# T5 attention followed by a feed-forward layer on one core: longer rows for q and k, full-width matmuls outside the scores, a band table through DRAM, paired score units and interleaved FFN products

## The chip, the cores and the metric

The kernel runs on one core of one Trainium2 chip. The metric is the device time of one execution in microseconds (us), lower is better. "TensorE", "VectorE", "ScalarE", "GpSimd" and "SyncE" are the engines; the profile writes PE, DVE, ACT, POOL and SP for them, and PEld for TensorE's weight loads. DRAM is the memory that holds the inputs, SBUF the on-chip memory that the engines work from, and PSUM the one that TensorE writes its products to; a DMA is a transfer, here between DRAM and SBUF or within SBUF. FFN is the feed-forward layer. "Before" and "after" are the two kernels.

## The reference

```python
# q, k, v: 8 batches x 8 heads x 576 tokens x 64; bias_table: 32 buckets x 8 heads
scores = (1/sqrt(64)) * q @ k^T
n      = abs(i - j)                      # distance of the two tokens
bucket = n if n < 16 else min(31, 16 + int(log(n/16)/log(128/16) * 15))
scores = scores + bias_table[bucket]     # one value per head and distance
attn   = exp(scores - rowmax);  attn = attn / rowsum
x      = attn @ v                        # -> 4608 tokens x 512
h      = x @ w_in                        # 512 -> 2048
g      = max(0.01 * h, h)                # leaky ReLU
out    = g @ w_out                       # 2048 -> 512, float32
```

Two properties matter. The bias is constant from distance 128 on, so after dividing by the constant it is a factor in a band of 128 tokens on each side of the diagonal and 1 elsewhere. And the 576 tokens are four blocks of 128 and one tail of 64, which is where narrow matmuls come from.

## The kernel before

Work goes by head pair: 32 pairs, numbered 0 to 31 here, four per batch. A pair has six score units (four blocks of 128 keys, one for the last 64 queries, one for the last 64 keys of both heads), an exponential on ScalarE per unit, a multiplication by the band table `eb` on VectorE, and two products with V ("AV"), one per head. The FFN is cut into 288 pieces of four 512-column matmuls, which are woven between the attention's matmuls, eight per pair.

The q and k loads take one token row of one head (64 numbers) at a time:

```python
    def load(b, h0, h1, by_head):
        i = b % NBUF
        for src, dst in ((q, qn[i]), (k, kn[i])):
            ...
                for c in range(NJ):
                    nc.gpsimd.dma_start(
                        out=dst[:, c, h0 * D : h1 * D].rearrange("s (h d) -> s h d", d=D),
                        in_=src[b, h0:h1, c * P : (c + 1) * P, :].rearrange("h s d -> s h d"),
                    )
        ...                                            # tails of 64 tokens apart; v likewise
```

The band table is built in 8 partitions, one per head, and spread from there to 128 partitions, each one element further to the left. The weights come after the loads of batch 0, and batch 1 comes after the weights:

```python
    ub = per.tile([H, UW], BF16, name="ub")            # 8 partitions x 512
    nc.vector.memset(ub, 1.0)
    ...                                                # 17 copies fill the band
    for h in range(H):
        r = ub[h : h + 1, :]
        eng = nc.sync if h % 2 == 0 else nc.scalar
        eng.dma_start(
            out=eb[:, h, :],
            in_=bass.AP(tensor=r.tensor, offset=r.offset + P - 1,
                        ap=[list(r.ap[0]), [-1, P], [1, 3 * P]]),
        )
    for e in range(2):
        nc.sync.dma_start(out=eb4[e * SL : (e + 1) * SL, :, :], in_=eb[0:SL, e::2, 0 : P + SL])
```

Score units use half of TensorE's rows (a head has 64 dimensions). Transposes of q and x, and AV, have a narrow last step for the tail:

```python
        nc.tensor.transpose(ps[:, NJ * P : S], in_=qn[i][0:SL, NJ, cols], identity=ident[0:SL, 0:SL])
    ...
            for e in range(2):                         # a score unit: two half-row matmuls
                r = slice(e * D, (e + 1) * D)
                nc.tensor.matmul(ps[:, e, :], lhsT=kt[r, u * P : (u + 1) * P], rhs=qt[r, 0:512],
                                 start=True, stop=True)
            nc.scalar.activation(at[:, :, u, 0:512], ps, AF.Exp, scale=scale)
    ...
        for ic in range(NJ + 1):                       # AV
            m = P if ic < NJ else SL
            cols = slice(ic * P, ic * P + m)
            for c in range(NJ):
                nc.tensor.matmul(ps[0:m, ic, :], lhsT=at[:, e, c, cols], rhs=vn[i][:, c, 2 * p + e, :],
                                 start=(c == 0), stop=False)
            nc.tensor.matmul(ps[0:m, ic, :], lhsT=at4[:, cols], rhs=v4[i][:, p, e, :],
                             start=False, stop=True)
```

The order of a pair, with `moe(k)` taking the next k pieces of the FFN from one queue (all of a tile's first product, then all of its second):

```python
        if p == 1 and b + 1 < B:
            load(b + 1, 0, H, False)
        if n == 0:
            load_weights()
        for u in range(NJ + 2):
            if n < N:
                qk_unit(n, u)
                band(n, u)
            if u == 1 and n > 0:
                av(n - 1, 0)
                moe(1)
            elif u == 3 and n > 0:
                av(n - 1, 1)
                moe(1)
            elif u == 4:
                moe(1)
                if n + 1 < N:
                    transposes(n + 1)
            elif u == 5:
                moe(1)
                if n > 0:
                    x_transposes(n - 1)
                    finished(n - 1)
            else:
                moe(2)
    moe(10 ** 9)
```

The softmax here doesn't subtract the row's maximum and nothing guards it: scores larger than these inputs give would overflow.

## Time and profile before

| | |
|---|---|
| time, median (lowest to highest) | 483.45 us (482.1 to 485.69), 4 runs |
| span of the profiled run | 481.7 us |
| first FFN matmuls and full TensorE from | about 85 us |
| steady time per head pair | 12.14 us |

The page of the kernel before opens with busy time per engine. In its second part a digit is the busy share, in tenths, of one of 40 slices of 12 us; the third part counts DMA packets, megabytes, and the share of all 16 DMA engines' time.

```profile
span 481.7 us, 9029 instructions
PE 427.3 (89%) x3808; PEld 214.1 (44%) x3808; DVE 193.6 (40%) x577; ACT 248.3 (52%) x338; POOL 122.5 (25%) x161
...
PE   2106837999999999999999999999999999999996
...
q0 software_dynamic: 115632, 18.36, 54.9%
```

TensorE comes and goes for the first 84 us and is full from there on. Its idle time is in the start.

Two stretches of the same kernel, the start and a steady pair. The columns are the stretch, its length, busy time with the number of instructions for PE, PEld, DVE, ACT and POOL, then the granted TensorE clock, the DMA share and GB/s.

```profile
0.00:85.00 85.00, 34.56 (x372) 19.47 (x372) 27.69 (x102) 26.80 (x32) 47.96 (x69) 0.90 1.51 113
182.00:194.33 12.33, 12.33 (x120) 6.18 (x117) 5.90 (x18) 9.04 (x14) 0.32 (x1) 1.00 0.50 50
```

TensorE works 34.56 of the first 85 us, while the DMA engines are busy (the DMA share reads 1.51; it is a sum over transfers and can pass 1). In the steady state it has no idle time, while ScalarE has 9.04 and VectorE 5.90 of 12.33 us. So a change in the steady state pays only if it shortens TensorE's own time.

From the chain of waits of the kernel before, the two longest DMAs that hold the start and one that follows them (start, duration, what):

```profile
11.42 27.23 DMA qn_100<-in_q_dram
...
48.40 19.92 DMA w_out_sb<-in_moe_w_out_dram
...
71.20 4.97 DMA kn_1_105<-in_k_dram
```

The last line is the tail of batch 1's k, which is issued behind the weights. Batch 1's q is too, and TensorE waits for it (in square brackets, the idle time before the matmul and what ended it):

```profile
69.20 0.29 PE L213 MATMUL ps_tq<-ident,qn_101 128*128 128x128 bf16 x1 [5.06 <-DMA qn_101<-in_q_dram]
```

From the timeline of TensorE before, around one pair. The columns are start, modelled duration, engine, line, operation, out<-in, rows*columns of the array in use, shape of the moving operand, count. Durations overlap, so the starts are what to read.

```profile
189.69 0.19 PE L287 MATMUL ps_o<-v_1_109,at_1979 128*128 128x65 bf16 x1
189.82 0.31 PE L285 MATMUL ps_o<-vn_107,at 128*64 128x65 bf16 x4
189.96 0.20 PE L287 MATMUL ps_o<-v_1_109,at_1979 128*64 128x65 bf16 x1
190.09 0.39 PE L313 MATMUL pm_2273<-xT_92,w_in_sb 128*128 128x512 bf16 x1
...
192.16 0.39 PE L213 MATMUL ps_tq<-ident,qn_101 128*128 128x128 bf16 x4
192.48 0.20 PE L214 MATMUL ps_tq<-ident,qn_101 64*128 64x64 bf16 x1
192.61 0.40 PE L219 MATMUL ps_tk<-ident,kn_103 128*128 128x128 bf16 x4
...
194.01 0.52 PE L302 MATMUL ps_tx<-ident,opair 128*128 128x128 bf16 x5
194.34 0.41 PE L237 MATMUL ps_s<-qt,kt 64*128 64x512 bf16 x2
```

Consecutive 65-column matmuls of the same width start 0.03 us apart. From the last 128*128 one (189.69) to the first 128*64 one (189.82) it is 0.13 us, and again 0.13 us on leaving (189.96 to 190.09). So each change of the array's width costs about 0.1 us beyond the streaming. The q tail shows it twice: four transposes of 128 columns stream in about 0.22 us, yet the 64*128 one starts 0.32 us after them, and 0.13 us passes until the next full one.

Two marks give the steady time per pair. These are the starts of the same matmul (score unit 5) of pairs 8 and 31 before; (411.35 - 132.07) / 23 = 12.14 us.

```profile
132.07 0.38 PE L251 MATMUL ps_s<-qt,kt 128*128 128x512 bf16 x1
...
411.35 0.38 PE L251 MATMUL ps_s<-qt,kt 128*128 128x512 bf16 x1
```

### The profile page before, as it was taken

What the parts mean: (1) busy time and instruction counts of PE and PEld (TensorE: products, weight loads), DVE (VectorE), ACT (ScalarE), POOL (GpSimd) and SP (SyncE); (2) the same over time, 40 slices, a digit from 0 to 9 for tenths busy, and PEclk for the clock granted to TensorE, in tenths of its full rate; (3) what the DMA queues carried; (4) which work ended last, traced back from release to release, by engine and by line L of the source; (5) the groups of instructions that cost most, each with busy time, mean ns of one, the idle gap of its engine ahead of it and who ended that gap; (6) DMA issues with size and microseconds to landing.
All of it is one profiled execution on the core that took longest, in us unless ns stands there. A gap on an engine that the chain in (4) does not pass through costs nothing.

```text
span 481.7 us, 9029 instructions
## 1 busy us (share of the span) xinstructions
PE 427.3 (89%) x3808; PEld 214.1 (44%) x3808; DVE 193.6 (40%) x577; ACT 248.3 (52%) x338; POOL 122.5 (25%) x161
## 2 busy tenths in 40 slices
PE   2106837999999999999999999999999999999996
PEld 0003514455555544555454555545555555544442
DVE  3102624444544454445444544454445444401101
ACT  1303624774477447754675467546754675152340
POOL 9127349506200721072107120703000000000000
PEclk9999876999999999999999999999999999999999
DMA  6999999909360926091809170927001000101101
GB/s 35 46 61 133 198 178 138 90 1 121 59 59 1 121 55 62 1 121 48 69 1 118 51 69 1 105 64 68 1 21 41 30 2 5 63 22 42 47 17 72
DMA packets 122817, 29.37 MB, mean 61 GB/s; under 512 B 114584, under 2 KB 117656, under 8 KB 122776
## 3 DMA queue, kind: packets, MB, share of 16 engines
q0 software_dynamic: 115632, 18.36, 54.9%
q1 hardware_dynamic: 6568, 10.03, 7.4%
q10 hardware_dynamic: 576, 0.39, 1.8%
q8 instruction: 30, 0.49, 0.4%
q14 instruction: 11, 0.09, 0.1%
HBM read 36.70 MB, written 9.44 MB: 96 GB/s over the span
## 4 chain that ended last, share of the span: by engine, by line
PE 82%; DMA 11%; POOL 4%; DVE 1%; issue 1%; ACT 1%; POOLq 0%
PE ps_o L285 10%; PE ps_s L237 7%; DMA qn_100<-in_q_dram 6%; DMA w_out_sb<-in_moe_w_out_dram 4%; PE ps_tx L302 2%; PE ps_o L287 2%; PE ps_tk L219 2%; PE ps_s L251 1%; PE ps_s L244 1%; PE ps_tq L213 1%; DMA kn_1_105<-in_k_dram 1%; PE pm_5235 L320 1%; PE pm_4729 L320 1%; PE pm_4043 L320 1%; PE pm_3880 L320 1%; PE pm_3357 L320 1%
## 5 line engine op out<-in xcount | busy, mean ns | idle before, releaser
L239 ACT ACTIVATE at<-ps_s 128x1024 bf16<-128x1024 f32 x128 | 129.4, 1022 | 72.2 <-PE ps_s L237 58.5
L271 DVE TENSOR_TENSOR at<-at,eb 128x768 bf16<-128x768 bf16 (+2 forms) x128 | 65.0, 508 | 135.4 <-ACT at L239 107.4
L320 PEld LDWEIGHTS <-gt 128*128 128x128 bf16 x576 | 49.8, 98 | 58.4 <-issue 6.0
L313 PEld LDWEIGHTS <-w_in_sb 128*128 128x128 bf16 x576 | 49.5, 98 | 58.5 <-issue 7.2
L285 PEld LDWEIGHTS <-at 128*128 128x128 bf16 (+1 forms) x1280 | 55.1, 102 | 23.4 <-issue 11.0
L237 PE MATMUL ps_s<-qt,kt 64*128 64x512 bf16 x256 | 52.2, 407 | 12.2 <-ACT at L239 10.5
L292 DVE TENSOR_TENSOR opair<-ps_o,rcp 128x256 bf16<-128x256 f32 (+1 forms) x128 | 41.0, 320 | 4.4
L285 PE MATMUL ps_o<-vn_106,at 128*128 128x65 bf16 (+1 forms) x640 | 34.7, 200 | 3.2 <-DVE opair L292 3.2
L291 DVE RECIPROCAL rcp<-ps_o 128x4 f32<-128x4 f32 (+1 forms) x128 | 21.0, 164 | 37.0 <-PE ps_o L287 37.0
L237 PEld LDWEIGHTS <-kt 64*128 64x128 bf16 x256 | 12.7, 95 | 50.4 <-issue 47.6
L285 PE MATMUL ps_o<-vn_107,at 128*128 128x65 bf16 (+1 forms) x640 | 32.8, 195 | 0.0
L111 POOL DMA_DIRECT2D qn_101<-in_q_dram x16 | 14.1, 896 | 67.2 <-PE ps_tq L214 61.7
L246 ACT ACTIVATE at<-ps_s 128x512 bf16<-128x512 f32 x32 | 19.1, 596 | 18.3 <-PE ps_s L244 18.3
L213 PE MATMUL ps_tq<-ident,qn_100 128*128 128x128 bf16 x64 | 7.5, 237 | 21.5 <-DMA qn_100<-in_q_dram 21.5
L111 POOL DMA_DIRECT2D qn_100<-in_q_dram x16 | 14.1, 926 | 45.7 <-PE ps_tk L220 22.9
L216 DVE COPY qt<-ps_tq 128x576 bf16<-128x576 bf16 x32 | 14.6, 456 | 26.3 <-PE ps_tq L214 26.3
L222 DVE COPY kt<-ps_tk 128x640 bf16<-128x640 bf16 x32 | 15.7, 490 | 8.0 <-PE ps_tk L220 8.0
L302 PEld LDWEIGHTS <-opair 128*128 128x128 bf16 (+1 forms) x160 | 12.9, 99 | 10.9 <-issue 0.5
L302 PE MATMUL ps_tx<-ident,opair 128*128 128x128 bf16 (+1 forms) x160 | 17.1, 220 | 0.0
L134 POOL DMA_DIRECT2D vn_107<-in_v_dram x16 | 14.1, 894 | 12.0 <-PE ps_o L287 11.5
L213 PEld LDWEIGHTS <-qn_100 128*128 128x128 bf16 x64 | 5.1, 104 | 25.1 <-DMA qn_100<-in_q_dram 17.1
L134 POOL DMA_DIRECT2D vn_106<-in_v_dram x16 | 14.0, 897 | 7.9 <-PE ps_o L287 7.4
(978 smaller groups left out, 772.8 us busy)
## 6 DMA issues: line engine op xcount, KB each, us to landing
out_dram<-y SPq DMA_DIRECT2D x36, 256.0 KB, 2.1
w_in_sb<-in_moe_w_in_dram POOLq DMA_DIRECT2D x4, 512.0 KB, 8.9
w_out_sb<-in_moe_w_out_dram POOLq DMA_DIRECT2D x4, 512.0 KB, 17.1
qn_101<-in_q_dram POOLq DMA_DIRECT2D x16, 128.0 KB, 4.2
kn_103<-in_k_dram POOLq DMA_DIRECT2D x16, 128.0 KB, 4.0
vn_107<-in_v_dram POOLq DMA_DIRECT2D x16, 128.0 KB, 4.3
qn_100<-in_q_dram POOLq DMA_DIRECT2D x12, 128.0 KB, 4.0
kn_102<-in_k_dram POOLq DMA_DIRECT2D x12, 128.0 KB, 4.2
```

The source lines that it names most:

```text
L111: nc.gpsimd.dma_start(out=dst[:, c, h0 * D : h1 * D].rearrange("s (h d) -> s h d", d=D), in_=src[b, h0:h1, c * P : (c + 1) * P, :].rearran ...
L134: nc.gpsimd.dma_start(out=vn[i][:, c, h0:h1, 0:D], in_=v[b, h0:h1, c * P : (c + 1) * P, :].rearrange("h s d -> s h d"),)
L237: nc.tensor.matmul(ps[:, e, :], lhsT=kt[r, u * P : (u + 1) * P], rhs=qt[r, 0:512], start=True, stop=True)
L239: nc.scalar.activation(at[:, :, u, 0:512], ps, AF.Exp, scale=scale)
L246: nc.scalar.activation(at[:, :, :, 512:S], ps[:, :, 0 : NJ * SL].rearrange("p e (c i) -> p e c i", i=SL), AF.Exp, scale=scale)
L271: nc.vector.tensor_tensor(out=o, in0=o, in1=m, op=ALU.mult)
L285: nc.tensor.matmul(ps[0:m, ic, :], lhsT=at[:, e, c, cols], rhs=vn[i][:, c, 2 * p + e, :], start=(c == 0), stop=False)
L291: nc.vector.reciprocal(rcp[0:rows, cs, :], ps[0:rows, cs, D : D + 1])
L292: nc.vector.tensor_tensor(out=opair[0:rows, cs, e * D : (e + 1) * D], in0=ps[0:rows, cs, 0:D], in1=rcp[0:rows, cs, :].to_broadcast([rows, ...
L302: nc.tensor.transpose(ps[:, ic * P : ic * P + m], in_=opair[0:m, ic, :], identity=ident[0:m, 0:m])
L313: nc.tensor.matmul(pm, lhsT=w_in_sb[:, c, f * P : (f + 1) * P], rhs=xT[c][:, t0 : t0 + TT], start=(c == 0), stop=(c == n_cc - 1))
L320: nc.tensor.matmul(pm, lhsT=gt[:, f, ts * P : (ts + 1) * P], rhs=w_out_sb[:, f, :], start=(f == 0), stop=(f == n_fc - 1))
```

## The change

Six things were changed together, all meant to raise TensorE's share. q and k are loaded six tokens per row, 384 contiguous numbers, so a batch needs 1,536 packets instead of 9,216; VectorE then puts the two heads of a pair side by side and undoes the token order when it copies the transposes out of PSUM. Outside the scores no matmul uses fewer than 96 of the array's rows: AV's last step reads 128 columns and the surplus is never used. The band table is built in all 128 partitions, written to DRAM, and read back with each partition's row one element further. Score units are issued two at a time. And the FFN's first product of one tile alternates, piece by piece, with the second product of another. The sixth is small in the code: batch 1's q and k are now issued ahead of the weights.

```diff
-    def load(b, h0, h1, by_head):
+    def load_qk(b, h0, h1):
         i = b % NBUF
+        for src, dst in ((q, qn[i]), (k, kn[i])):
+            nc.gpsimd.dma_start(
+                out=dst[0:RQ, h0:h1, :, :].rearrange("r h c d -> r h (c d)"),      # RQ = 96
+                in_=src[b, h0:h1, :, :].rearrange("h (r c) d -> r h (c d)", c=NC), # NC = 6
+            )
  ... (load_v keeps the old form; kn4 and its fill are gone)

-    ub = per.tile([H, UW], BF16, name="ub")
+    ub = per.tile([P, H, UW], BF16, name="ub")
     nc.vector.memset(ub, 1.0)
  ... (the same copies, now on 128 partitions x 8 heads)
-    for h in range(H):
-        r = ub[h : h + 1, :]
-        eng = nc.sync if h % 2 == 0 else nc.scalar
-        eng.dma_start(out=eb[:, h, :], in_=bass.AP(tensor=r.tensor, offset=r.offset + P - 1,
-                        ap=[list(r.ap[0]), [-1, P], [1, 3 * P]]))
+    urows = nc.dram_tensor("u_rows", [P, H, UW], BF16, kind="Internal")
+    for h0, h1 in ((0, 2), (2, H)):
+        nc.sync.dma_start(out=urows.ap()[:, h0:h1, :], in_=ub[:, h0:h1, :])
+    for h0, h1 in ((0, 2), (2, H)):
+        nc.sync.dma_start(
+            out=eb[:, h0:h1, :],
+            in_=bass.AP(tensor=urows, offset=h0 * UW + P - 1, ap=[[H * UW - 1, P], [UW, h1 - h0], [1, 3 * P]]),
+        )
  ... (eb4 likewise from urows)

+    def pair_rows(n, which):                           # VectorE: the two heads of a pair side by side
+        t = pr_pool.tile([RQ, NC, 2 * D], BF16, name="pr")
+        nc.vector.tensor_copy(out=t.rearrange("r c (e d) -> r c e d", e=2),
+                              in_=src[b % NBUF][0:RQ, 2 * p : 2 * p + 2, :, :].rearrange("r e c d -> r c e d"))
+    def transpose_q(n):
+        for c in range(NC):
+            nc.tensor.transpose(ps[:, c * RQ : (c + 1) * RQ], in_=qs[0:RQ, c, :],
+                                identity=ident[0:RQ, 0:RQ])
+        nc.vector.tensor_copy(out=qt.rearrange("p (r c) -> p r c", c=NC),
+                              in_=ps[:, 0:S].rearrange("p (c r) -> p r c", c=NC))
  ... (transpose_k likewise)

         for ic in range(NJ + 1):                       # AV
-            m = P if ic < NJ else SL
-            cols = slice(ic * P, ic * P + m)
             for c in range(NJ):
-                nc.tensor.matmul(ps[0:m, ic, :], lhsT=at[:, e, c, cols], rhs=vn[i][:, c, 2 * p + e, :],
+                o = (e * NJ + c) * S + ic * P
+                nc.tensor.matmul(ps[:, ic, :], lhsT=at[:, o : o + P], rhs=vn[i][:, c, 2 * p + e, :],
                                  start=(c == 0), stop=False)
  ... (the step with at4 likewise; x_transposes without its narrow tail)

+            if n == 0:                                 # order of the first loads
+                load_qk(1, 0, H)
+                load_weights()
+                load_v(1, 0, H, False)
+            ps_a, ps_b = qk_mm(n, 0), qk_mm(n, 1)      # score units in pairs
+            exp_band(n, 0, ps_a)
+        moe(1)
+        if live:
+            exp_band(n, 1, ps_b)
  ... (units 2, 3 and 4, 5 likewise)

     def moe(n_pieces):
-        while queue and n_pieces: ... next(queue[0]) ...
+        for _ in range(n_pieces):
+            piece(("in", "out")[turn], False)          # skipped when that product has nothing ready
+            turn ^= 1
```

## The prediction

> **What bounds the kernel now.** Three stretches (table by stages, timeline). (1) 0 to about 85 us, start-up: TensorE waits. The chain of waits runs here through DMAs: the batch-0 q load (27 us), the w_out load (20 us), the batch-1 k tail (5 us). The first exponentials start at 18.2 us, because ScalarE was issuing band-table DMAs; TensorE is busy 0.8 of 10 us in 30-40. Batch-1 q and k land at 69 to 76 us behind the weights. (2) 85 to 412 us, steady state: TensorE is busy 12.33 of 12.33 us per head pair (182-194.33), ScalarE 9.0, VectorE 5.9, clock 1.00. (3) 412 to 482 us: FFN alone, 3.45 us per 16 matmuls, 216 ns each.
>
> **What the steady state consists of.** Eight FFN pieces of 4 x 216 ns are 6.9 us of about 12.2; attention takes 5.3. Reading starts of neighbouring matmuls: a pair of half-row score matmuls streams in 0.22 us but occupies 0.32, with about 0.1 us lost going in and again coming out. The same 0.1 us appears around the 64-column attention-times-V matmuls and the 64-row transposes. The Trainium skill ("TensorEngine Tiling (Array Packing)", Key Properties) says changing the tiling mode drains TensorE; the trace agrees, at about 0.1 us. I count about 17 such changes per head pair: 5 score groups (10), two AV tails (4), q tail (2), x tail (1).
>
> **What the change does.** Changes fall from 17 to 6 (three score groups), saving about 1.1 us per head pair. Streaming work stays: six 96-column transposes replace four 128s and a tail. Steady state: 12.2 to about 11.1 us, TensorE-bound. VectorE gains pair-row copies and strided q/k copies; I estimate 7 us of 11, off the critical path. Interleaving both FFN products evens ScalarE (4 instead of 0 or 8 leaky-ReLU passes) but removes no TensorE work; during the first tile only 4 pieces per pair run, leaving 78 instead of about 56 to 64 for the tail.
>
> Start-up: q and k go from 9,216 packets of 64 elements per batch to 1,536 of 384. The 256-byte reads ran at about 1,000 packets per us (24,269 in 70 to 94 us), so a batch takes 14 us now, about 10 to 12 then. The band table no longer comes from single SBUF partitions (16.8 us to landing) and ScalarE issues none of it; but VectorE must build it on 128 partitions (the fill alone about 4 us, estimated from 0.48 us for 512 elements), then out and back through DRAM: first bands about 18 us. Then about 6.6 us per pair; batch 1's v lands behind the weights, estimated 52 to 57 us. So the steady phase begins near 53 instead of 85 us.
>
> **Sum.** 53 + 4 pairs x 8 + 23 x 11.1 + last pair 9 + 78 x 0.865 + 3.5 = 420; plus 5 for new stalls: **425 us**, range 410 to 446. Faster by over 2%: 0.96; within 2%: 0.03; slower: 0.01.
>
> **What would show it.** Steady pair 11.1 us with TensorE full; no gap around AV; queue-0 packets near 52,000; first FFN matmul near 50 us; tail about 70 us of 216 ns matmuls.
>
> **What would make it wrong.** 96-row transposes draining too (+0.4 us a pair, +13 us); VectorE lateness (strided copies, larger ops) stalling TensorE through the three shared PSUM buffers, one now held by the interleaved second product; the DRAM round trip landing after 25 us; batch 1's v after 65 us.

## The result and the profile after

| | before | after |
|---|---|---|
| time, median (lowest to highest) | 483.45 us (482.1 to 485.69) | 439.62 us (439.09 to 439.96) |
| ratio, 95% | | 0.9088 (0.9053 to 0.9124) |

There were four runs of each. A ratio is the mean time of one kernel's runs over that of the other's of the same rounds, so it is not quite the ratio of the medians. The result is right.

The page after, same lines:

```profile
span 438.2 us, 9059 instructions
PE 392.3 (90%) x3872; PEld 202.3 (46%) x3872; DVE 229.1 (52%) x581; ACT 247.1 (56%) x338; POOL 60.8 (14%) x84
...
PE   0511888999999999999999999999999999999996
...
q0 software_dynamic: 52960, 18.36, 37.6%
```

The same 18.36 MB went through the load queue in less than half the packets (a slice is now 11 us). TensorE is at 0.8 from the fifth slice (44 us) on and full from about 77 us; before, it came and went until 84 us. The stages of the kernel after:

```profile
0.00:68.50 68.50, 29.06 (x386) 17.23 (x386) 39.04 (x115) 26.94 (x32) 28.15 (x43) 1.00 1.14 165
68.50:102.40 33.90, 31.48 (x405) 18.14 (x405) 24.45 (x63) 28.29 (x40) 6.06 (x9) 1.00 0.52 54
281.50:292.60 11.10, 11.10 (x120) 5.74 (x119) 6.75 (x17) 7.40 (x11) 0.00 (x0) 1.00 0.28 55
366.00:438.20 72.20, 68.13 (x316) 30.71 (x314) 8.30 (x12) 19.07 (x32) 0.00 (x0) 1.00 0.13 48
```

The steady pair is again 11.10 of 11.10 us TensorE, with VectorE's longer copies (6.75 us, from 5.90) still far from the limit. The last stretch is 79 pieces of the FFN (316 matmuls) and nothing else.

Where the time went, by the starts of score unit 5 of pairs 4, 8 and 31 in the two profiled runs:

| stretch | before | after | difference |
|---|---|---|---|
| start to pair 4 | 83.5 | 65.5 | -18.0 |
| pair 4 to 8 | 48.5 | 34.6 | -14.0 |
| pair 8 to 31 (23 pairs) | 279.3 | 253.8 | -25.4 |
| pair 31 to the end | 70.4 | 84.3 | +13.9 |
| span | 481.7 | 438.2 | -43.5 |

The second and fourth rows cancel. With alternating products a pair gives the FFN only four pieces while the first tile's second product is not ready, so 16 pieces of 0.865 us = 13.8 us leave pairs 5 to 8 and come back at the end. The gain is the start, 18 us, and the steady state, 25.4 us.

The marks of pairs 9 and 31 after, 243.36 us apart, 11.062 us per pair. (Before, by the same two marks, it was 12.141.)

```profile
110.56 0.39 PE L253 MATMUL ps_s<-qt,kt_109 128*128 128x512 bf16 x1
...
353.92 0.39 PE L253 MATMUL ps_s<-qt,kt_109 128*128 128x512 bf16 x1
```

The timeline of TensorE after, in a steady pair:

```profile
284.31 0.61 PE L244 MATMUL ps_s<-qt,kt_109 64*128 64x512 bf16 x4
284.85 0.39 PE L327 MATMUL pm_4181<-xT_92,w_in_sb 128*128 128x512 bf16 x1
...
286.34 0.29 PE L301 MATMUL ps_o<-vn_104,at_110 128*128 128x65 bf16 x4
286.47 0.19 PE L303 MATMUL ps_o<-v_0_106,at_0_112 128*128 128x65 bf16 x1
286.50 0.42 PE L227 MATMUL ps_tk<-ident,pr 96*128 96x96 bf16 x6
286.75 1.03 PE L338 MATMUL pm_4097<-w_out_sb,gt 128*128 128x512 bf16 x4
```

AV's last step runs on at 0.03 us per matmul. The 96-row transposes start 0.03 us after it, and the next 512-column matmul starts 0.25 us later, which is their streaming time (6 x 96 columns): no width change is visible around 96 rows. The four half-row matmuls of two units take 0.54 us with one change behind them.

From the chain of waits after, the start (start, duration, what):

```profile
4.15 3.47 DVE ub L156
...
11.56 8.22 DMA u_rows<-ub
...
21.51 20.77 DMA eb_99<-u_rows
```

And from the waits after, the two that VectorE's band multiplications spent on the table (engine, tile, line <- releaser: total us, count, mean):

```profile
DVE at_110 L288 <- DMA eb<-u_rows: 14.0, 1, 14.0
DVE at_0_112 L288 <- DMA eb_99<-u_rows: 9.9, 1, 9.9
```

The start is now held by the table's way through DRAM: filled at 7.6 us, finished at 11.2, written by 19.8 (1 MB, while q, k and v are arriving), read back by 28.9 for the first two heads and by 42.3 for the tail table `eb4` (shown as `eb_99`). What the reads met between 30 and 42 us is shown by the DMA queues of that window (packets, MB, share of 16 engines). q0 carries the weights, q1 the table.

```profile
q0 software_dynamic: 1203, 1.95, 87.4%
q1 hardware_dynamic: 1164, 0.66, 25.0%
```

Nearly equal numbers of packets went through, but one of q0's is on average three times as large. The Trainium skill ("DMA: Bandwidth & Descriptors", Queues, rings and completion order) says that each DMA engine takes turns between queue rows packet by packet. The equal counts agree with turns (in the trace a packet is about one contiguous row: 52,960 packets for 51,712 rows of q, k, v and weights; the page's holds several descriptors). So the table, with short rows, got 0.66 of the 2.61 MB beside the weights.

### The profile page after: what moved, and what is told of

It reads as the page before. It is cut to its first block, busy times and chain, and to the rows that moved or that the text cites. A ratio compares the mean times of both kernels' runs of the same rounds, so it can differ in the third digit from the quotient of the medians.

```text
span 438.2 us, 9059 instructions
## 1 busy us (share of the span) xinstructions
PE 392.3 (90%) x3872; PEld 202.3 (46%) x3872; DVE 229.1 (52%) x581; ACT 247.1 (56%) x338; POOL 60.8 (14%) x84
## 3 DMA queue, kind: packets, MB, share of 16 engines
q0 software_dynamic: 52960, 18.36, 37.6%
## 4 chain that ended last, share of the span: by engine, by line
PE 79%; DVE 7%; DMA 7%; ACT 5%; issue 2%; SPq 0%; DVEq 0%; ACTq 0%
PE ps_o L301 7%; PE ps_s L244 6%; DMA eb_99<-u_rows 5%; PE ps_s L253 2%; DMA u_rows<-ub 2%; PE ps_o L303 2%; ACT at_110 L264 2%; ACT at_111 L264 2%; PE ps_tx L315 2%; PE ps_tq L216 1%; PE ps_tk L227 1%; PE ps_s L250 1%; DVE at_110 L288 1%; DVE opair L307 1%; ACT gt L329 1%
## 5 line engine op out<-in xcount | busy, mean ns | idle before, releaser
L264 ACT ACTIVATE at_111<-ps_s 128x1024 bf16<-128x1024 f32 x64 | 64.7, 1021 | 38.4 <-PE ps_s L244 38.3
L264 ACT ACTIVATE at_110<-ps_s 128x1024 bf16<-128x1024 f32 x64 | 64.3, 1021 | 20.6 <-PE ps_s L244 20.4
L288 DVE TENSOR_TENSOR at_110<-at_110,eb 128x512 bf16<-128x512 bf16 (+1 forms) x64 | 32.3, 506 | 53.0 <-ACT at_110 L264 36.8
L288 DVE TENSOR_TENSOR at_111<-at_111,eb 128x512 bf16<-128x512 bf16 (+1 forms) x64 | 32.3, 506 | 44.1 <-ACT at_111 L264 40.0
L244 PE MATMUL ps_s<-qt,kt_109 64*128 64x512 bf16 x128 | 20.8, 396 | 13.7 <-DVE kt_109 L230 13.1
L301 PEld LDWEIGHTS <-at_110 128*128 128x128 bf16 x640 | 28.3, 100 | 10.0 <-DVE opair L307 3.0
L307 DVE TENSOR_TENSOR opair<-ps_o,rcp 128x320 bf16<-128x320 f32 x64 | 31.5, 492 | 2.2
L301 PEld LDWEIGHTS <-at_111 128*128 128x128 bf16 x640 | 27.2, 98 | 9.9 <-DVE opair L307 3.0
L216 PE MATMUL ps_tq<-ident,pr 96*128 96x96 bf16 x192 | 14.2, 212 | 11.5 <-DVE pr L208 11.5
L244 PE MATMUL ps_s<-qt,kt_108 64*128 64x512 bf16 x128 | 21.6, 403 | 2.3 <-DVE kt_108 L230 1.2
L303 PE MATMUL ps_o<-v_0_106,at_0_112 128*128 128x65 bf16 x80 | 13.7, 200 | 8.9 <-DVE at_0_112 L288 8.8
L303 PEld LDWEIGHTS <-at_0_112 128*128 128x128 bf16 x160 | 15.9, 99 | 9.2 <-DVE at_0_112 L288 9.2
L306 DVE RECIPROCAL rcp<-ps_o 128x5 f32<-128x5 f32 x64 | 12.2, 191 | 11.4 <-PE ps_o L303 11.4
L244 PEld LDWEIGHTS <-kt_109 64*128 64x128 bf16 x128 | 4.2, 94 | 28.1 <-issue 13.8
L301 PE MATMUL ps_o<-vn_104,at_110 128*128 128x65 bf16 x320 | 15.8, 200 | 0.9 <-DVE opair L307 0.8
L123 POOL DMA_DIRECT2D vn_105<-in_v_dram x16 | 14.1, 888 | 15.5 <-PE ps_o L303 7.6
L301 PE MATMUL ps_o<-vn_104,at_111 128*128 128x65 bf16 x320 | 14.5, 194 | 1.7 <-DVE opair L307 1.7
L216 PEld LDWEIGHTS <-pr 96*128 96x128 bf16 x192 | 10.0, 101 | 12.5 <-DVE pr L208 12.4
L303 PEld LDWEIGHTS <-at_1_113 128*128 128x128 bf16 x160 | 15.6, 97 | 0.2 <-DVE at_1_113 L288 0.2
```

Of the source, the lines that this page charges most:

```text
L123: nc.gpsimd.dma_start(out=vn[i][:, c, h0:h1, 0:D], in_=v[b, h0:h1, c * P : (c + 1) * P, :].rearrange("h s d -> s h d"),)
L216: nc.tensor.transpose(ps[:, c * RQ : (c + 1) * RQ], in_=qs[0:RQ, c, :], identity=ident[0:RQ, 0:RQ])
L288: nc.vector.tensor_tensor(out=o, in0=o, in1=m, op=ALU.mult)
L301: nc.tensor.matmul(ps[:, ic, :], lhsT=at[:, o : o + P], rhs=vn[i][:, c, 2 * p + e, :], start=(c == 0), stop=False)
L303: nc.tensor.matmul(ps[:, ic, :], lhsT=at4[:, ic * P : (ic + 1) * P], rhs=v4[i][:, p, e, :], start=False, stop=True)
L306: nc.vector.reciprocal(rcp, ps[:, :, D : D + 1])
```

## The experiments

Each kernel is the kernel after with the edit shown. All gave right results, and each was timed in three rounds against the kernel before on the same chip (four runs of it, seven or eight of before). "Ratio" is to before; after has 0.9088. The experiments ran in groups on two chips, so between groups the ratios are compared. Differences from after that are given in us are between medians; by the ratios they come out 0.4 to 1.2 us higher.

| kernel | median us (lowest to highest) | ratio, 95% |
|---|---|---|
| one_unit | 447.97 (447.88 to 448.17) | 0.927 (0.9248 to 0.9293) |
| tails64 | 458.2 (458.15 to 458.52) | 0.9482 (0.9463 to 0.9502) |
| old_packets | 439.27 (438.26 to 441.48) | 0.9095 (0.9064 to 0.9127) |
| old_band | 451.94 (451.63 to 452.84) | 0.9354 (0.9333 to 0.9376) |
| band_first | 426.74 (425.94 to 427.12) | 0.8834 (0.882 to 0.8848) |
| band_first_short | 439.88 (439.66 to 440.45) | 0.911 (0.9097 to 0.9124) |
| no_mix | 439.2 (439.06 to 439.77) | 0.9097 (0.9083 to 0.911) |
| band_first_v | 426.96 (426.52 to 428.48) | 0.8851 (0.8831 to 0.8872) |
| band_early | 430.44 (429.8 to 430.63) | 0.8908 (0.8887 to 0.893) |
| band_early_fill | 432.43 (430.94 to 433.31) | 0.8951 (0.8917 to 0.8985) |
| band_early_v | 420.09 (418.18 to 421.44) | 0.8694 (0.8656 to 0.8733) |
| band_early_v_fill | 418.95 (418.59 to 419.96) | 0.8675 (0.8648 to 0.8703) |

### The steady state: one_unit and tails64

The theory is that each change of the array's width costs 0.1 us of TensorE and that the whole steady gain is the number of changes taken away. The rival is that the gain comes from something else in the steady state, such as ScalarE being fed better. `one_unit` issues the score units singly again (two more groups, so four more changes per pair):

```diff
-            ps_a, ps_b = qk_mm(n, 0), qk_mm(n, 1)
-            exp_band(n, 0, ps_a)
+            exp_band(n, 0, qk_mm(n, 0))
         moe(1)
         if live:
-            exp_band(n, 1, ps_b)
+            exp_band(n, 1, qk_mm(n, 1))
  ... (units 2 and 3 likewise)
```

> The changed kernel with its score units issued one at a time again; all other parts stay. Theory (mode changes): four more changes of the tiling mode per head pair at about 0.1 us each, with TensorE still busy without a break: the steady pair goes from 11.09 to about 11.5 us, the time up by 9 to 14 us. Rival (the pairs matter because they keep ScalarE fed, not because of TensorE's modes): matmul streaming stays at 11.1 us a pair and TensorE shows idle time waiting for ScalarE, or, if that wait was hidden before, the time changes by less than 3 us.

`tails64` brings back the 64-token tails of AV and of the x transposes (six more changes per pair), and with them VectorE's normalisation in two calls:

```diff
         for ic in range(NJ + 1):
+            m = P if ic < NJ else SL
...
-                nc.tensor.matmul(ps[:, ic, :], lhsT=at[:, o : o + P], rhs=vn[i][:, c, 2 * p + e, :],
+                nc.tensor.matmul(ps[0:m, ic, :], lhsT=at[:, o : o + m], rhs=vn[i][:, c, 2 * p + e, :],
...
-            nc.tensor.transpose(ps[:, ic * P : (ic + 1) * P], in_=opair[:, ic, :], identity=ident)
+            nc.tensor.transpose(ps[:, ic * P : ic * P + m], in_=opair[0:m, ic, :], identity=ident[0:m, 0:m])
```

> The changed kernel with 64-column attention-times-V matmuls and the 64-row x transpose put back for the last 64 tokens (and VectorE's normalisation split in two calls as it was before). Theory: six more mode changes per head pair at 0.1 us: steady pair about 11.7 us, time up by 13 to 19 us. Rival (a narrower matmul does less work, and what costs is only the number of matmuls): no change or slightly faster, within 3 us, since the number of matmuls is the same.

Measured: one_unit is 8.4 us slower than after, tails64 18.6 us slower. The marks of pairs 9 and 31 in one_unit:

```profile
109.10 0.39 PE L253 MATMUL ps_s<-qt,kt 128*128 128x512 bf16 x1
...
361.81 0.39 PE L253 MATMUL ps_s<-qt,kt 128*128 128x512 bf16 x1
```

And in tails64:

```profile
113.96 0.39 PE L253 MATMUL ps_s<-qt,kt 128*128 128x512 bf16 x1
...
371.38 0.39 PE L253 MATMUL ps_s<-qt,kt 128*128 128x512 bf16 x1
```

The pair takes 252.71 / 22 = 11.487 us in one_unit, 0.425 more than after, so 0.106 per change; and 257.42 / 22 = 11.701 us in tails64, 0.639 more, so 0.1065 per change. Two edits of different kind give the same price per change. Nor does TensorE wait for ScalarE: in the steady pairs of both (240 to 270 us) its timeline shows no wait for another engine. So the theory stands. The total of one_unit is a little below what was expected because pairs 5 to 8, which TensorE does not fill, are faster with single units: 8.05 us each against 8.48 after, where the timeline shows the paired units waiting 0.26 to 0.31 us for ScalarE to free a score buffer. The steady loss of 23 x 0.425 = 9.8 us less 4 x 0.43 = 1.7 us is 8.1 us.

### The start: old_packets and old_band

Each undoes one half of what was changed in the start. `old_packets` loads q and k in rows of 64 numbers again, into the same places:

```diff
-            nc.gpsimd.dma_start(
-                out=dst[0:RQ, h0:h1, :, :].rearrange("r h c d -> r h (c d)"),
-                in_=src[b, h0:h1, :, :].rearrange("h (r c) d -> r h (c d)", c=NC),
-            )
+            for c in range(NC):
+                nc.gpsimd.dma_start(
+                    out=dst[0:RQ, h0:h1, c, :],
+                    in_=src[b, h0:h1, :, :].rearrange("h (r c) d -> r h c d", c=NC)[:, :, c, :],
+                )
```

> The changed kernel with the same row layout of q and k, but loaded in 64-element pieces again (six transfers for each one). Packets of queue 0 go from about 53,000 to about 114,000. Theory (after the change, the start is held by the band table and not by q and k): steady pair unchanged at 11.1 us, the first steady pair starts a few us later, time up by 3 to 10 us. Rival (the long rows are what shortened the start): the start goes back to about 85 us, time up by 15 us or more.

`old_band` builds and spreads the table as the kernel before does:

```diff
-    ub = per.tile([P, H, UW], BF16, name="ub")
+    ub = per.tile([H, UW], BF16, name="ub")
...
-    urows = nc.dram_tensor("u_rows", [P, H, UW], BF16, kind="Internal")
-    ... (two writes, two reads)
+    for h in range(H):
+        r = ub[h : h + 1, :]
+        eng = nc.sync if h % 2 == 0 else nc.scalar
+        eng.dma_start(out=eb[:, h, :], in_=bass.AP(tensor=r.tensor, offset=r.offset + P - 1,
+                        ap=[list(r.ap[0]), [-1, P], [1, 3 * P]]))
```

> The changed kernel with the band table built on 8 partitions and spread from single SBUF partitions as before. Theory (those transfers were what slowed everything in the first 40 us of the kernel before): bands for the first pair early, but the whole table only near 35 to 40 us, q, k and v delayed with it, first steady pair 5 to 12 us later than 68.5, time up by 5 to 12 us. Rival (the trip through DRAM with 1 MB written is no better than the old way): time within 3 us or even faster.

Measured: old_packets costs nothing (439.27 against 439.62), which neither theory expected. Its timeline shows why the total hides the rows. The score unit of pair 4 comes at 55.7 us, 10 us earlier than after, and the table is no longer late: GpSimd has more loads to issue (174 instructions in all instead of 84), so the first weights are issued at 38.0 us instead of 14.1, and the table's reads land 3.7 and 7.3 us after issue instead of 9.0 and 18.4. (The reads are still in SyncE's queue and were issued at about 17 us, so they were over before the first weights.) That the one follows from the other is supported by band_first below. But batch 1's v is late with the weights, and TensorE waits for it:

```profile
65.60 0.21 PE L302 MATMUL ps_o<-vn,at 128*128 128x65 bf16 x1 [5.62 <-DMA vn<-in_v_dram]
```

One limit went and another came at almost the same place. Undoing a part in one place of a chain with two limits close to each other can't price it; that needed the next pair.

old_band is 12.3 us slower than after, at the slow edge of what was expected. Its chain of waits shows a single-partition read and, behind it, the copy of the tail table:

```profile
11.29 29.90 DMA eb<-ub
42.01 13.94 DMA eb<-eb
```

The whole table lands at about 41 us and its tail at 56 us. In after the first two heads' part lands at 28.9 us, the rest at about 38.7 and the tail at 42.3. So the way through DRAM is the better of the two, although it is what holds the start of after. But the single-partition reads end only 2.5 us later than the whole table of after; most of the 12.3 us is the tail, which old_band copies out of the finished table (13.9 us, beside the weights) and after reads from DRAM beside the rest. The Trainium skill ("SBUF — State Buffer", Door 1: The DMA port swizzle) says that DMA bandwidth depends on how many of the SBUF's 16 ports the partitions reach; a source of one partition reaches one. The slow read agrees in direction, but it shared the DMA engines with the loads and the mechanism was not separated.

### Taking the table out of the weights' way: band_first and band_first_short

If the table's reads are slow because they share the DMA engines with the weights, they should go ahead of the weights in the same queue. `band_first` moves them, and batch 1's q and k, to that place:

```diff
+    def load_band():
         for h0, h1 in ((0, 2), (2, H)):
-        nc.sync.dma_start(
+            nc.gpsimd.dma_start(                       # the same reads, from GpSimd's queue
                 out=eb[:, h0:h1, :], ...
+    load_qk(1, 0, H)
+    load_band()
     pair_rows(0, "q")
...
             if n == 0:
-                load_qk(1, 0, H)
                 load_weights()
```

> The changed kernel with the band table's reads from DRAM moved onto the queue that carries q, k, v and the weights, ahead of the weights, so that the weights can't be served before them. Theory (the reads landed at 28.9 and 42.4 us because they shared the DMA engines with 8.4 MB of weights): all tables landed by about 30 us, pair 1 starts near 30 instead of 43.6 us, the first interleaved pair limited then by batch 1's v, near 58 to 62 us; time down by 6 to 12 us, to 427 to 434. Rival (the reads are slow in themselves, 768-byte rows from DRAM): tables no earlier than 38 us, time within 3 us of 439.

`band_first_short` is band_first with the short rows of old_packets, so that rows are priced where the table is not the limit.

> band_first with q and k loaded in 64-element pieces again. Theory (the long rows were worth nothing in the changed kernel only because the band table held the start; with that out of the way they shorten the queue ahead of the table, the weights and v): 6 to 15 us slower than band_first. Rival (long rows are worth nothing at all, POOL and the engines keep up with short ones): within 3 us of band_first.

Measured: band_first has ratio 0.8834 and is 12.9 us under after (12.3 by the ratios), just past the better edge of what was expected. Its chain of waits:

```profile
11.54 7.83 DMA u_rows<-ub
...
19.97 6.41 DMA eb<-u_rows
```

The write of the larger part is nearly as slow as in after (8.2 us), but the read of the first two heads now takes 6.4 us (9.0 from issue to landing after) and lands at 26.4 us, and pair 4 comes at 52.9 us instead of 65.5. So the reads met contention with the weights. band_first alone doesn't show it, for it also moves the reads from SyncE's queue to GpSimd's; but in old_packets they stayed in SyncE's and, ahead of the weights, landed in 3.7 and 7.3 us, so the queue isn't the cause. band_first_short is 13.1 us slower than band_first on the same chip: that is the price of short rows when the table does not hide it. So the table's new way (its tail included) is worth 12.3 us in after, and the long rows 13.1 us in band_first, but nothing in after, where the table limits.

### The interleaving alone: no_mix

`no_mix` takes the FFN's pieces in the old order (one product of one tile after the other) and leaves the rest:

```diff
     def moe(n_pieces):
         for _ in range(n_pieces):
-            piece(("in", "out")[turn], False)
-            turn ^= 1
+            if running["out"] is not None or made["in"] > made["out"]:
+                piece("out", True)
+            else:
+                piece("in", True)
```

> The changed kernel with the two FFN products in one queue again, 8 pieces in every pair from the first tile on. Theory (TensorE is full either way, the interleaving only moves work to the tail): time within 4 us of 439.6; 64 pieces or fewer left for the tail, pairs 5 to 8 about 11.5 us instead of 8.5. Rival (the interleaving evens ScalarE and keeps TensorE from waiting): pairs with 8 leaky-ReLU passes take 12 us or more and the time rises by 5 us or more.

Measured: 439.2 us, within 0.4 us of after. The marks tell how it evens out. From pair 4 to pair 9 it takes 56.4 us instead of 45.0, as every pair has its eight pieces; 22 steady pairs take 11.148 us each instead of 11.062, so 1.9 us more; and the end after pair 31 is 14.3 us shorter. Interleaving is worth 1.9 us in the steady pairs and loses 2.4 us in those that it leaves half filled: 16 pieces, 13.8 us, left them, and they became only 11.4 us shorter, with waits for ScalarE's score buffers (above). Its effect on the total is nil within the noise.

### Which limit comes next: four orders of the first loads

After band_first the candidates for the next limit were batch 1's v, which waits behind the weights, and the table itself. `band_first_v` puts v ahead of w_out:

```diff
                 load_weights()                         # w_in only
                 load_v(1, 0, H, False)
+                load_w_out()
```

> band_first with batch 1's v loaded between w_in and w_out (w_out is first read three pairs later). Theory (after the table, v is the next to end last): first interleaved pair about 48 to 52 us, another 6 to 11 us faster than band_first, about 418 to 425 in all. Rival (something else, VectorE's or ScalarE's pace in the first pairs, holds the start): within 3 us of band_first.

`band_early` writes the table as two DRAM tensors, so that heads 0 and 1 don't wait for the write of the others, issues v of batch 0 (pairs 1 to 3) behind the table's reads, and moves batch 1's q and k behind that:

```diff
     load_qk(0, 2, H)
-    load_v(0, 2, H, False)
...
+        ur = nc.dram_tensor(f"u_rows{h0}", [P, h1 - h0, UW], BF16, kind="Internal")
+        nc.sync.dma_start(out=ur.ap(), in_=ub[:, h0:h1, :])
...
+    load_band()
+    load_v(0, 2, H, False)
+    load_qk(1, 0, H)
```

> band_first with the band table kept as two DRAM tensors, so that the read for the first two heads waits for their own write alone, and with all table reads ahead of pairs 1 to 3's v and of batch 1's q and k on the queue. Theory (in band_first the write at 11.5 to 19.5 us and the read to 26.5 us are slow because v, q and k share the engines): first bands near 18 instead of 26.5 us, every later step earlier by as much, about 418 to 422 us. Rival (the 6 to 8 us are what such a write and read take, or v arriving later now holds pair 2): first bands no earlier than 23 us, time within 3 us of 426.7.

`band_early_fill` also fills only the parts of the table outside the band:

```diff
-    nc.vector.memset(ub, 1.0)
+    nc.vector.memset(ub[:, :, 0:P], 1.0)
+    nc.vector.memset(ub[:, :, 3 * P - 1 : UW], 1.0)
```

> band_early with VectorE filling only the 257 of 512 columns of the table that nothing else writes. The fill took 3.47 us; about half goes, on the chain that ends with the first bands: 1 to 2 us faster than band_early. If the table's data from DRAM, not VectorE, comes last by then, or the first fill was hidden behind the bias table's own load (landed near 4.3 us), no change within 1 us.

`band_early_v` is band_early with v ahead of w_out, and `band_early_v_fill` has both.

> band_early with batch 1's v loaded between w_in and w_out. In band_early the fourth pair's scores were 8 us earlier than in band_first (44.6 against 52.9 us), but the fifth's were 64.7 us, behind batch 1's v, which lay behind both weights. Theory (with the table early, v ends last): fifth pair near 53 to 55 us, time 416 to 421 us. Rival (the time of the fifth pair is not v's): within 3 us of 430. The same move was worth nothing in band_first, where the table came last.

> band_early_v with the shorter fill. Theory (VectorE's table building is on the chain again once v is out of the way): 1 to 2 us faster than band_early_v. Rival (the v of the first batch, which is now queued behind all the table's reads, or the DMA queue as a whole, ends last): no change within 1 us, or slower, as band_early_fill was against band_early (by 2 us).

Measured: band_first_v is the same as band_first, where 6 to 11 us had been expected, so v did not limit there. band_early reaches pair 4 at 44.6 us, 8 us ahead of band_first, and is nevertheless slower (0.8908 against 0.8834); it missed what was expected of it. Its chain of waits, and from its timeline a matmul that waits:

```profile
10.81 2.79 DMA u_rows<-ub
...
25.95 16.36 DMA w_in_sb<-in_moe_w_in_dram
...
43.30 14.93 DMA vn<-in_v_dram
```

```profile
53.95 0.22 PE L305 MATMUL ps_o<-vn,at 128*128 128x65 bf16 x1 [5.09 <-DMA vn<-in_v_dram]
```

The write of the first two heads now takes 2.8 us, where it landed 6.7 us after issue in after and the reads had to wait for the larger one as well. But everything that was moved ahead of the weights pushed batch 1's v back, and TensorE waits for it; pair 5's score unit comes at 64.7 us, against 62.0 in band_first. TensorE's granted clock was also lower behind that wait (0.50 from 55 to 60 us and 0.61 from 60 to 65, where band_first has 1.00), and what of the loss is due to it was not separated. band_early_fill saves time before the table and loses it there: 2 us slower than band_early, a miss for the same reason. band_early_v gives v its place and now gains 2.4% over band_early (0.8694), as expected. There the table is the limit again, this time its second part:

```profile
18.30 5.60 DMA eb<-u_rows
```

Once v is no longer waited for, the smaller fill is 1.1 us faster (418.95 against 420.09), but the runs of the two overlap, so that last step is unclear. band_early_v_fill is the best version: 0.8675 of before, and by the ratios 4.5% under after. The same edit, v ahead of w_out, was worth nothing in band_first and 10 us in band_early.

A version with an 8 KB table in DRAM, one row per head, was not measured. So it is open whether a smaller table would land sooner still.

## Why the prediction was right or wrong

The direction and the range held: 439.6 us lies between 410 and 446. The centre of 425 us was 14.6 us low, and the range held partly by luck: the 5 us set aside for new stalls covered a third of a miss in the start. Its sum, term by term (the measured numbers are from the profiled run, whose span of 438.2 us is a little less than its time of 439.96):

| term of the prediction | predicted | measured |
|---|---|---|
| steady phase begins | 53 | 68.5 |
| next four pairs | 4 x 8 = 32 | 33.9 |
| 23 steady pairs | 23 x 11.1 = 255.3 | 23 x 11.06 = 254.4 |
| last pair, 78 pieces, end | 9 + 67.5 + 3.5 = 80 | 81.4 |
| allowance for new stalls | 5 | in the rows above |
| sum | 425 | 438.2 |

**The step that failed** is "first bands about 18 us" and with it "the steady phase begins near 53". Bands began at 28.9 us and the tail table came at 42.3, so the phase began at 68.5. The table was finished at 11.2 us, so the predicted 18 left about 7 us for both ways through DRAM; the write alone took 8.2 us beside q, k and v, and the reads 9 and 20.8 us beside the weights. It had named this as what could make it wrong ("the DRAM round trip landing after 25 us"). band_first and old_packets show that the reads' share is contention: with the reads ahead of the weights, in GpSimd's queue, the whole kernel became 12.9 us faster, and in SyncE's queue the reads became as short. In band_early, with a table in two tensors and v of batch 0 behind its reads, the first bands began at 17.2 us, the predicted time; the total did not follow, since v was late then. With v ahead of w_out as well (band_early_v) pair 5's score unit comes at 54.9 us, 19.8 us before that of after, and the time is 420.1 us, the prediction's sum without its allowance.

**The steady state was right**: 11.1 us predicted, 11.06 measured. The count behind it was one off. I had counted 17 changes before and 6 after; the trace has 16 and 6. The x tail adds none in the kernel before, since the next matmuls after it are half-row scores: 0.33 us pass from the transposes at 194.01 to the scores at 194.34, which is the streaming of 576 columns (0.24 us) and one change, and the scores would have needed that one anyway. Ten changes of 0.1065 us are 1.065 us; the marks give 1.079. The Trainium skill ("TensorEngine Tiling (Array Packing)", Key Properties) says that changing the tiling mode drains TensorE. The traces agree, and one_unit and tails64 put the price at 0.106 us.

**Wide transposes** were named as a risk ("96-row transposes draining too"). The timeline shows no gap around them, and the period leaves no room for one.

**VectorE lateness** was the other risk. It did not come: 6.75 of 11.10 us busy against an estimate of 7, and the allowance of 5 us for new stalls was not needed in the steady state. The permuted copy out of PSUM is slower, 748 ns against 456 ns for the same 576 columns. The Trainium skill ("VectorE: DVE Perf Modes", What auto-detection actually checks) asks a step of one in every tensor for the doubled rate on 16-bit data, which the strided side does not have; the two durations agree with it, and off the critical path it cost nothing.

**The rows of q and k** did what was predicted of packets (52,960 in the load queue, about 52,000 predicted), but their worth could not be read from after. It is 13.1 us between band_first and band_first_short and nothing between after and old_packets.

**The first FFN matmul** came at 66.2 us, not near 50, by the same failed step. **Interleaving** was rightly predicted to remove no TensorE work and to leave about 78 pieces for the end; that it costs 1.9 us in pairs 5 to 8 (33.9 instead of 32) was not foreseen, and no_mix shows the total even.

What stays open: how much of the kernel before's 85 us start was the single-partition table, how much the short rows, and how much batch 1's q and k behind the weights; the first two were only undone from after, and the third was undone in no run, though TensorE waited for it at 69 us. Open too is how much of the start of before is due to its lower granted clock (0.90 in the mean of the first 85 us, 1.00 in after).

## What to carry to other kernels

Price the steady state by counting what TensorE pays outside streaming, then check it with two undo experiments of different kind, since a cost per change that both agree on can be multiplied out. In a start-up with several DMA chains close together, a part is worth only what the next limit leaves: undoing one showed nothing here, and the same reordering was worth nothing in one version and 10 us in another. A small transfer that the first computation waits for should be issued ahead of the large ones: here the tail table's pieces took about 20 us beside the weights and 7.4 us ahead of them.

## What the Trainium skill lacked or had wrong

- "TensorEngine Tiling (Array Packing)" says that a mode change drains TensorE but gives no duration. Here it is 0.106 us per change (0.425 us for four in one_unit, 0.639 us for six in tails64).
- The same page lists modes of 128, 64 and 32 rows and doesn't say what a tile of 96 rows does. Here six transposes of 96 rows between 128-row matmuls show no gap (286.47, 286.50, 286.75 us).
- "DMA: Bandwidth & Descriptors" tells of the turns between queues but not of what follows for unequal rows: 1,203 packets of one queue moved 1.95 MB while 1,164 of the other moved 0.66 MB. Its advice that spreading loads over the issuing engines brings no bandwidth leaves out what it means for an urgent transfer beside loads that another engine has issued before it: up to 20.8 us for the 96 KB pieces of the tail table in after, 7.4 us in band_first, where they go ahead of the weights.
- "SBUF — State Buffer" tells that few partitions reach few ports, but its measured table starts at four partitions (one port, 1 MiB) and has no figure for a source of one partition. Here eight reads of 96 KB, each from a single partition, landed 16.8 us (SyncE's) and 17.8 us (ScalarE's) after issue in the kernel before, and the chain of old_band has one of 29.9 us, both beside other loads; 192 KB from DRAM rows took 6.4 us in band_first.
